# Packing the 64-row tails of a top-k attention and Fourier mixing kernel into shared 128-wide blocks, on one Trainium2 core

## The chip, the cores and the metric

The kernel runs on one core of one Trainium2 chip. The time is the device time of one execution in microseconds (us). Before the change the median of four runs is 2020.8 us (2019.78 to 2022.19). One execution was also taken with the hardware profiler; its rows carry the durations used below.

## The reference, cut to what matters

There are 8 batches of 8 heads, 576 positions and 64 features per head, all in float32. Each query keeps its 32 largest scores; then come a softmax, a product with `v`, a real Fourier mix over positions and channels, a layer norm and a two-layer MLP.

```python
scores = scale * np.matmul(q, k.transpose(0, 1, 3, 2))
kth = np.partition(scores, -top_k, axis=-1)[..., -top_k:-top_k + 1]
scores = np.where(scores >= kth, scores, -1000000000.0)
attn = np.exp(scores - np.max(scores, axis=-1, keepdims=True))
attn = attn / (np.sum(attn, axis=-1, keepdims=True) + 1e-09)
x = heads_side_by_side(np.matmul(attn, v))        # (8, 576, 512)
mixed = np.real(np.fft.fft(np.fft.fft(x, axis=1), axis=2))
u = x + mixed
ch = np.maximum(layer_norm(u) @ w_ch1, 0.0) @ w_ch2
return u + ch
```

## The kernel before

**Tiles.** 576 positions are four full blocks of 128 and a tail of 64 (32 rows from each half of the sequence). Two heads are handled together as a pair, one in partitions 0 to 63 and the other in 64 to 127 of the transposed `q` and `k`; there are 32 pairs, four per batch. A pair has nine *items* (`IN_PAIR`, L259): for each full query block one item for each head (`e` 0 and 1), and one item with the 64 tail queries of both heads stacked to 128 rows (`e` None). That makes 288 items.

**One item** passes these stations. TensorE (PE) makes its scores in PSUM (`scores`, L267: part 0 against the 512 full keys, one matmul per head, L296; part 1 against the 64 tail keys of both heads at once through the block-diagonal `kt_t`, L285), and ScalarE (ACT) copies them to an `S` tile (L299, L289). VectorE (DVE) finds the 32 largest with four MAX8 and three MATCH_REPLACE8 (L313, L315). GpSimd (POOL) makes the two bounds from them (`bounds`, L322). ACT makes a penalty with a Relu that reads the bound (L329), POOL subtracts it (L330); both are `mask`. ACT takes the exponential (L336). PE transposes the result in blocks of 128 columns (`transposes`, L355: four blocks and then one more for the tail, in a PSUM tile of its own), ACT copies the blocks to `PT` (L357), and for every 5 or 4 items PE multiplies with `v` (`attend`, L371).

**The loop.** `while` at L915 runs one step per item, and everything is issued in the order written there. In step i PE makes the scores of item i+3, spreads in *units* of the MLP of the previous batch (`hidden`, L659; `back`, L674 and L699), and transposes item i-2. DVE does the last rounds of item i and the first of item i+1. POOL gets `bounds(i)` (L1006), then what the plan put under "pool" (L1013), and in the next step the subtraction of item i. In the first 36 steps (the first batch) latencies are shorter by one step, no MLP is there yet, and DVE, ACT and POOL also convert the weights.

**Folds.** Before the Fourier matmuls of a batch (`dft_tokens`, L506) the rows of `x` are folded by four operations for each of two parities (`fold_ops`, L446, all through L462). For batches 1 to 6 they are on POOL, under "pool": one operation per step from step T0 and from T0+6 (L844), for batch 1 two per step from T0 and T0+3 (L837). The matmuls of parity 0 follow at T0+5 (T0+3 for batch 1).

**Preparation.** `prep` (L232) transposes `q` of the next pair at step 0 of a pair and `k` at step 5, each in five blocks, the last with 64 rows and zeros. Both come through the one `nat_t` buffer, loaded on SyncE's queue (SP) by L215 and L217. In the first batch `prep` uses the PSUM tiles "mm" (three banks, shared with the weight conversion); scores use "sp" (two banks).

**End of the MLP.** `back` leaves a block in PSUM; ACT scales it into `ct` (L680, a tile of the `W` ring that also holds the items' working rows), POOL adds it to `x` (L682; DVE in the last batch), SP stores it (L686). The 64-row tail block ends on DVE one step later (L713, L714).

`level` and `fixed_cost` (L873 to L891) share the MLP units out over the steps by an estimate of the PE time of each step.

Of the kernel before, what the change touches and what calls it, by code (L numbers as in the profile page):

```python
# [59 lines left out]
def kernel(  # L60
# [60 lines left out]
    kt_t = const.tile([P, P], F32, name="kt", tag="kt")  # L121
# [78 lines left out]
    nat, qT_of, kT_of, v_of, PT, Ssb, Wk, M8, Nt = ({} for _ in range(9))  # L200
# [5 lines left out]
    def load_heads(dst, src, pair, tail0=0, queues=None):  # L206
        b, hp = divmod(pair, NPB)
        for tails in range(2):
            queue = (queues or (nc.sync, nc.sync))[tails]
            for e in range(2):  # L210
                s2 = src[b, 2 * hp + e].rearrange("(h r) d -> h r d", h=2)
                for h in range(2):
                    r0 = tail0 + TH * h
                    if tails:
                        queue.dma_start(out=dst[r0:r0 + TH, NF, e, :], in_=s2[h, 2 * P:HS, :])  # L215
                    else:
                        queue.dma_start(  # L217
                            out=dst[:, 2 * h:2 * h + 2, e, :],
                            in_=s2[h, 0:2 * P, :].rearrange("(t p) d -> p t d", p=P),
                        )  # L220

    def load_nat(n, pair, dst=None, queues=None):
        if pair < NPAIR:
            nat[n, pair] = nat_t if dst is None else dst
            load_heads(nat[n, pair], q if n == "q" else k, pair, 0, queues)

    def load_v(pair):
        if pair < NPAIR:
            v_of[pair] = v_t[pair % 2]
            load_heads(v_of[pair], v, pair, TAIL)  # L230

    def prep(n, pair, pool=ps_t, tag="tp"):  # L232
# [5 lines left out]
        for c0, c1 in ((0, NF), (NF, NC)):  # L238
# [5 lines left out]
            if c0 == 0:  # L244
                dst, got = t_sb[:, 0:NF * P], tp.rearrange("p a c -> p (a c)")
            else:
                dst, got = t_sb[:, NF * P:], tp[:, 0, 0:TAIL]
            if n == "q":
                nc.scalar.mul(out=dst, in_=got, mul=scale)
            elif c0 == 0:  # L250
                nc.scalar.copy(out=dst, in_=got)
            else:
                for hd in (slice(0, D), slice(D, P)):
                    nc.scalar.copy(out=kt_t[hd, hd], in_=got[hd])
# [12 lines left out]
    def scores(i, part):  # L267
# [7 lines left out]
        rows, keys = ROWS[t], slice(0, NF * P)  # L275
        if part == 0:
            for n in range(1 if e is None else 2):
                Ssb[i + n] = attp.tile([P, S], F32, name=f"S_{i + n}", tag="S", bufs=6)

        to = [(Ssb[i], slice(TAIL * h, TAIL * (h + 1))) if e is None  # L280
              else (Ssb[i + h], slice(0, P)) for h in range(2)]
        q_cols = slice(P * t, P * t + rows)
        if part == 1:
            sp = ps_s.tile([P, NF * P], F32, name=f"sp_{i}_t", tag="sp")
            nc.tensor.matmul(  # L285
                sp[0:rows, 0:P], lhsT=qT[:, q_cols], rhs=kt_t, start=True, stop=True
            )
            for h, (s_t, r) in enumerate(to):
                nc.scalar.copy(  # L289
                    out=s_t[r, NF * P:S], in_=sp[0:rows, TAIL * h:TAIL * (h + 1)]  # L290
                )
            return 0.3
        for h, (s_t, r) in enumerate(to):
# [8 lines left out]
    def top_ops(i, rounds):  # L302
# [3 lines left out]
        if i not in Wk:  # L306
            Wk[i] = attp.tile([P, S], F32, name=f"wk_{i}", tag="W", bufs=5)
            M8[i] = small.tile([P, TOPK], F32, name=f"m8_{i}", tag="m8", bufs=5)
# [9 lines left out]
    def bounds(i):  # L318

        if i < N:  # L320
            Nt[i] = small.tile([P, 2], F32, name=f"nt_{i}", tag="nt", bufs=6)
# [19 lines left out]
    def transposes(i):  # L341
        pair, t, e = items[i]
        p_sb = Wk.pop(i)
        ch, col = CHUNK_OF[t]
        if (pair, ch) not in PT:
            PT[pair, ch] = attp.tile(
                [P, 2, NC, CW[ch]], F32, name=f"PT_{pair}_{ch}", tag=f"PT{ch}", bufs=1
            )
        pt = PT[pair, ch]
        dsts = [(e, 0, P)] if e is not None else [(0, 0, TAIL), (1, TAIL, TAIL)]  # L350
        for c0, c1 in ((0, NF), (NF, NC)):
            tp = ps_t.tile([P, 4, P], F32, name=f"tpP_{i}_{c0}", tag="tp")
            for c in range(c0, c1):
                k0 = min(P * c, S - P)
                nc.tensor.transpose(tp[:, c - c0, :], p_sb[:, k0:k0 + P], ident)  # L355
            for he, o, w in dsts:
                nc.scalar.copy(  # L357
                    out=pt[:, he, c0:c1, col:col + w], in_=tp[:, 0:c1 - c0, o:o + w]
                )
        return 0.6  # L360

    def attend(pair, ch, c0=0, c1=None):
# [6 lines left out]
        for c in range(NC):  # L369
            for e in range(2):  # L370
# [3 lines left out]
                    rhs=pt[:, e, c, c0:c1],  # L374
# [5 lines left out]
    def attended(pair, ch, late):  # L380
# [14 lines left out]
        rd = small.tile([P, 6], F32, name=f"rd_{pair}_{ch}", tag="rd", bufs=6)  # L395
# [205 lines left out]
    def stats(b, t):  # L601
        rows, mvb = ROWS[t], mv[b % 2]
        st6 = small.tile([P, 6], F32, name=f"st6_{b}_{t}", tag="st6")
# [44 lines left out]
    def mlp_units(b):  # L648
        x = x_of[b]
        last = b == B - 1  # L650
        hTs = {}

        def hidden(ch, it):
            w, unT = CW[ch], unT_of[b, ch]
            if ch not in hTs:
                hTs[ch] = batp.tile([P, NIT, CW[0]], F32, name=f"hT_{b}_{ch}", tag="hT")
            hp = ps_m.tile([P, CW[0]], F32, name=f"hp_{b}_{ch}_{it}", tag="mm")
# [5 lines left out]
            nc.scalar.activation(out=hTs[ch][:, it, 0:w], in_=hp[:, 0:w], func=AF.Relu)  # L663

        cps = {}

        def back(ch, t, part):
            n, hT, rs = CHUNKS[ch].index(t), hTs[ch], rs_of[b]
# [3 lines left out]
            if t != 4:  # L672
# [5 lines left out]
                if part == 7:  # L678
                    ct = attp.tile([P, DM], F32, name=f"ct_{b}_{t}", tag="W", bufs=5)
# [375 lines left out]
```

## Time and profile before

| what | value |
|---|---|
| median of four runs | 2020.8 us |
| the profiled execution | 2020.43 us |
| its span in the trace | 2018.7 us |
| PE busy | 1890.4 us (94%) |
| DVE busy | 1626.8 us (81%) |
| ACT busy | 1225.3 us (61%) |
| POOL busy | 852.2 us (42%) |
| L355 transposes of P on PE | 1440, mean 286 ns |
| L357 copies to PT on ACT, 128x128 form | 256, mean 278 ns |
| L296 scores of tail queries, 64x512 form | 128, mean 688 ns |

PEld is the loading of weights into TensorE, which overlaps PE. A row that begins with a line number is a group of equal instructions: line, engine, operation, output from input, count, then total busy time and the mean of one. In rows of the timeline the first two numbers are start and duration in us. "A <- B" in a list of waits means that A could go on when B had ended. A matmul in float32 shows as two records.

### The profile page before, as it was taken

To read this page: it belongs to the slowest core of one execution; us is meant where nothing else is said; L and a number is where in the kernel's file an instruction comes from. 1 tells how busy PE (TensorE), PEld (TensorE's weight loads), DVE (VectorE), ACT (ScalarE), POOL (GpSimd) and SP (SyncE) were. 2 spreads that over 40 slices of the span, in tenths; PEclk is the share of its full clock that TensorE was granted. 3 is DMA by queue.
4 is the path that set the end of the run, shared out by engine and by line. 5 is a ranking of instruction groups with operands and counts; after the bars stand their busy time and mean duration, and the time that the engine had idled before them with its cause. 6 is when DMAs were issued, how large, how long until landed. Compare 5 with 4: busy or idle time off the path is not lost.

```text
span 2018.7 us, 27736 instructions
## 1 busy us (share of the span) xinstructions
PE 1890.4 (94%) x8642; PEld 1142.9 (57%) x8642; DVE 1626.8 (81%) x3374; ACT 1225.3 (61%) x3059; POOL 852.2 (42%) x1143
## 2 busy tenths in 40 slices
PE   5667689999899999999999999999999999998999
PEld 3434356565565566647565656647565656556655
DVE  7998898999899999989889888888889888853100
ACT  6877737676676667657666666656666666651111
POOL 4869822334733265224632464225632454223100
PEclk8777679999899999999999999999999999999999
DMA  4323100010000100000000001000000001000000
GB/s 129 97 84 95 54 7 19 24 26 24 23 19 24 27 24 24 18 23 21 24 24 13 26 18 29 18 24 22 22 24 24 20 13 35 1 13 1 11 14 11
DMA packets 133587, 57.84 MB, mean 29 GB/s; under 512 B 124352, under 2 KB 124480, under 8 KB 133440
## 3 DMA queue, kind: packets, MB, share of 16 engines
q1 hardware_dynamic: 132208, 55.73, 10.2%
q8 instruction: 70, 1.15, 0.2%
q14 instruction: 77, 0.63, 0.1%
q10 hardware_dynamic: 1232, 0.33, 0.1%
HBM read 46.57 MB, written 9.44 MB: 28 GB/s over the span
## 4 chain that ended last, share of the span: by engine, by line
PE 78%; DVE 7%; ACT 5%; POOL 5%; issue 4%; DMA 0%; SPq 0%; POOLq 0%; DVEq 0%; ACTq 0%
PE hp L659 23%; PE cp L674 20%; PE o L371 7%; PE sp L296 7%; PE tpP L355 6%; PE mp L576 3%; PE yp L520 3%; PE cp L699 3%; DVE m L313 3%; DVE wk L315 2%; PE sp_t L285 2%; POOL wk L330 2%; POOL w L192 1%; PE cm L801 1%; ACT wk L336 1%
## 5 line engine op out<-in xcount | busy, mean ns | idle before, releaser
L330 POOL TENSOR_TENSOR wk<-S,wk 128x576 f32<-128x576 f32 x288 | 406.6, 1412 | 865.6 <-ACT wk L329 775.2
L313 DVE MAX8 m<-wk 128x8 f32<-128x576 f32 x864 | 623.1, 749 | 5.6
L659 PE MATMUL hp<-unT,w 128*128 128x256 f32 (+1 forms) x2048 | 538.6, 410 | 2.2 <-POOL t L625 2.2
L674 PE MATMUL cp<-w,hT 128*128 128x512 f32 x1024 | 479.2, 599 | 0.0
L659 PEld LDWEIGHTS hp<-unT,w 128*128 128x128 f32 x2048 | 374.5, 191 | 126.6 <-issue 31.8
L315 DVE MATCH_REPLACE8 wk<-m,wk 128x576 f32<-128x576 f32 x576 | 427.6, 742 | 0.0
L357 ACT COPY PT<-tpP 128x512 f32<-128x512 f32 (+3 forms) x640 | 221.4, 408 | 128.3 <-PE tpP L355 125.2
L674 PEld LDWEIGHTS cp<-w,hT 128*128 128x128 f32 x1024 | 179.4, 190 | 189.7 <-issue 188.9
L336 ACT ACTIVATE wk<-wk,nt 128x576 f32<-128x576 f32 x288 | 226.2, 785 | 78.3 <-POOL wk L330 77.1
L355 PE MATMUL tpP<-ident,wk 128*128 128x128 f32 x1440 | 219.7, 286 | 53.2 <-ACT wk L336 47.8
L355 PEld LDWEIGHTS tpP<-ident,wk 128*128 128x128 f32 x1440 | 173.7, 146 | 152.0 <-ACT wk L336 71.7
L313 DVE MAX8 m<-S 128x8 f32<-128x576 f32 x288 | 214.2, 744 | 36.9 <-ACT S L289 36.5
L329 ACT ACTIVATE wk<-S,nt 128x576 f32<-128x576 f32 x288 | 227.3, 789 | 10.5 <-POOL nt L322 8.7
L663 ACT ACTIVATE hT<-hp 128x320 f32<-128x320 f32 (+1 forms) x256 | 104.6, 409 | 194.3 <-PE hp L659 193.0
L299 ACT COPY S<-sp 128x512 f32<-128x512 f32 (+1 forms) x320 | 173.9, 586 | 74.2 <-PE sp L296 72.9
L315 DVE MATCH_REPLACE8 wk<-m,S 128x576 f32<-128x576 f32 x288 | 213.6, 742 | 0.0
L371 PE MATMUL o<-PT,v 128*64 128x256 f32 (+3 forms) x1440 | 196.9, 417 | 10.0 <-ACT PT L357 9.7
L296 PE MATMUL sp<-kT,qT 64*128 64x512 f32 (+1 forms) x640 | 198.4, 683 | 1.8 <-ACT means L811 1.7
L371 PEld LDWEIGHTS o<-PT,v 128*64 128x64 f32 x1440 | 111.7, 153 | 84.9 <-issue 15.0
L192 POOL TENSOR_TENSOR w<-w,space 128x512 f32<-128x512 f32 x96 | 123.5, 1286 | 5.9 <-ACT space L183 3.4
L682 DVE TENSOR_TENSOR x<-x,ct 128x512 f32<-128x512 f32 x4 | 2.8, 692 | 130.9 <-ACT ct L680 130.9
L420 DVE TENSOR_TENSOR x<-tpx,rd 128x256 f32<-128x256 f32 x64 | 27.2, 424 | 82.7 <-PE tpx L416 77.0
(111 smaller groups left out, 1737.3 us busy)
## 6 DMA issues: line engine op xcount, KB each, us to landing
space<-in_moe_w_ch_dram SPq DMA_DIRECT2D x32, 512.0 KB, 3.5
nat<-in_q_dram SPq DMA_DIRECT2D x128, 64.0 KB, 2.0
v<-in_v_dram SPq DMA_DIRECT2D x128, 64.0 KB, 2.1
out_dram<-x SPq DMA_DIRECT2D x32, 256.0 KB, 2.1
nat<-in_k_dram SPq DMA_DIRECT2D x124, 64.0 KB, 2.0
nat<-in_q_dram SPq DMA_DIRECT2D x128, 8.0 KB, 1.7
v<-in_v_dram SPq DMA_DIRECT2D x128, 8.0 KB, 1.7
nat<-in_k_dram SPq DMA_DIRECT2D x124, 8.0 KB, 1.6
```

What stands on the lines that cost most here:

```text
L296: nc.tensor.matmul(sp[r], lhsT=qT[hd, q_cols], rhs=kT[hd, :], start=True, stop=True)
L299: nc.scalar.copy(out=s_t[r, keys], in_=sp[r])
L313: ops.append(lambda src=src, m8=m8: nc.vector.max(out=m8, in_=src))
L315: ops.append(lambda src=src, m8=m8: nc.vector.match_replace(w, m8, src, NEG))
L329: nc.scalar.activation(out=w, in_=Ssb[i], func=AF.Relu, scale=-FAR, bias=Nt[i][:, 1:2])
L330: nc.gpsimd.tensor_tensor(out=w, in0=Ssb.pop(i), in1=w, op=ALU.subtract)
L336: nc.scalar.activation(out=w, in_=w, func=AF.Exp, bias=Nt.pop(i)[:, 0:1], accum_out=den_t[pair % 3][:, c:c + 1],)
L355: nc.tensor.transpose(tp[:, c - c0, :], p_sb[:, k0:k0 + P], ident)
L357: nc.scalar.copy(out=pt[:, he, c0:c1, col:col + w], in_=tp[:, 0:c1 - c0, o:o + w])
L371: nc.tensor.matmul(o[D * e:D * (e + 1), c0:c1], lhsT=vv[:, c, e, :], rhs=pt[:, e, c, c0:c1], start=(c == 0), stop=(c == NC - 1),)
L659: nc.tensor.matmul(hp[:, 0:w], lhsT=w1[:, dt, P * it:P * (it + 1)], rhs=unT[:, dt, 0:w], start=(dt == 0), stop=(dt == NDT - 1),)
L674: nc.tensor.matmul(cp, lhsT=hT[:, it, P * n:P * (n + 1)], rhs=w2[:, it, :], start=(it == 0), stop=(it == NIT - 1),)
```

## The change

The change has seven parts.

1. *P tails of two heads.* The working rows of the two items (t, 0) and (t, 1) lie side by side in one tile, `[P, 2, S]`, three buffers instead of five single ones. The second head's scores are stored with the 64 tail keys first. So the tails of both heads are 128 adjacent columns, transposed as one block when the second head's item is done. `PT` has 9 blocks instead of 10; the tail halves of `v` are placed to match, with zeros in the other half.
2. *Tails of q and k.* The 64 tail rows of `k` are loaded below those of `q`, by the loads for `q`; one transposed block gives both. `kt_t` has two copies. `k` is left with four blocks.
3. *Tail queries' scores.* Instead of two matmuls with 512 columns there are four with 256, on the four quarters of the PE array (64 rows by 64 columns); ACT copies four pieces instead of two.
4. *Folds.* Under a new name "pool0" they are issued ahead of `bounds(i)` instead of behind it. Those of parity 0 move one step later, for batch 1 those of both parities.
5. *End of the MLP.* `ct` leaves the `W` ring for the fold buffer "fold_s" and for free columns of `hT`, which is packed closely for the shorter chunk. The block t = 3 (and all of the last batch) is finished by one DVE instruction from PSUM, for batches 0 to 6 one step later.
6. *First batch.* `prep` takes its PSUM tiles from "sp" instead of "mm".
7. *Smaller rings* for `m8` (5 to 3), `nt` (6 to 4), `rd` (6 to 4) and `st6` (4 to 2), and changed costs in `fixed_cost`.

```diff
...
+            if n == "q":
+                load_tails(nat[n, pair], q, pair, (0, 0))
+                load_tails(nat[n, pair], k, pair, (TAIL, TAIL))
...
-            load_heads(v_of[pair], v, pair, TAIL)
+            load_full(v_of[pair], v, pair)
+            load_tails(v_of[pair], v, pair, (0, TAIL))
...
-        for c0, c1 in ((0, NF), (NF, NC)):
+        for c0, c1 in ((0, NF), (NF, NC)) if n == "q" else ((0, NF),):
...
+                nc.scalar.mul(out=t_sb[:, NF * P:], in_=got[:, 0:TAIL], mul=scale)
                 for hd in (slice(0, D), slice(D, P)):
-                    nc.scalar.copy(out=kt_t[hd, hd], in_=got[hd])
+                    nc.scalar.copy(out=kt_t[pair % 2][hd, hd], in_=got[hd, TAIL:P])
...
+        if e is None:
+            half = NF * P // 2
+            sps = [
+                ps_s.tile([P, NF * P], F32, name=f"sp_{i}_{h}", tag="sp") for h in range(2)
+            ]
+            for g in range(2):
+                for h in range(2):
+                    hd = slice(D * h, D * (h + 1))
+                    nc.tensor.matmul(
+                        sps[h][TAIL * g:TAIL * (g + 1), 0:half],
+                        lhsT=qT[hd, q_cols], rhs=kT[hd, half * g:half * (g + 1)],
+                        start=True, stop=True,
+                    )
+            for h, (s_t, r, _, _) in enumerate(to):
+                for g in range(2):
+                    nc.scalar.copy(
+                        out=s_t[r, half * g:half * (g + 1)],
+                        in_=sps[h][TAIL * g:TAIL * (g + 1), 0:half],
+                    )
+            return 0.6
...
-            Wk[i] = attp.tile([P, S], F32, name=f"wk_{i}", tag="W", bufs=5)
-            M8[i] = small.tile([P, TOPK], F32, name=f"m8_{i}", tag="m8", bufs=5)
+            e = items[i][2]
+            if e != 1:
+                Wp[i] = attp.tile([P, 2, S], F32, name=f"wk_{i}", tag="W", bufs=3)
+            Wk[i] = Wp[i - 1][:, 1, :] if e == 1 else Wp[i][:, 0, :]
+            M8[i] = small.tile([P, TOPK], F32, name=f"m8_{i}", tag="m8", bufs=3)
...
+        def full():
+            k0 = TAIL if e == 1 else 0
+            tp = ps_t.tile([P, 4, P], F32, name=f"tpP_{i}", tag="tp")
+            for c in range(NF):
+                nc.tensor.transpose(tp[:, c, :], p_sb[:, k0 + P * c:k0 + P * (c + 1)], ident)
...
+        def tails():
+            tp = ps_t.tile([P, 4, P], F32, name=f"tpP_{i}_t", tag="tp")
+            if e == 1:
+                both = Wp.pop(i - 1).rearrange("p e s -> p (e s)")[:, NF * P:S + TAIL]
+                nc.tensor.transpose(tp[:, 0, :], both, ident)
+                nc.scalar.copy(out=pt[:, 2 * NF, col:col + P], in_=tp[:, 0, :])
+                return
...
+        full()
+        if e != 0:
+            tails()
+        return 0.48 if e == 0 else 0.6
...
-                    rhs=pt[:, e, c, c0:c1],
+                    rhs=pt[:, 2 * NF if c == NF else NF * e + c, c0:c1],
...
+                    def finish():
+                        nc.vector.scalar_tensor_tensor(
+                            out=xt, in0=cp, scalar=rs[:, t:t + 1], in1=xt, op0=ALU.mult, op1=ALU.add
+                        )
+
+                    if last:
+                        finish()
+                    elif t == 3:
+                        late_next.append(finish)
+                    else:
+                        ct = ct_of(t)
+                        nc.scalar.mul(out=ct, in_=cp, mul=rs[:, t:t + 1])
+                        nc.gpsimd.tensor_tensor(out=xt, in0=xt, in1=ct, op=ALU.add)
...
-                        at(T0 + 3 * par + n // 2, "pool", op)
+                        at(T0 + 3 * par + n // 2 + 1, "pool0", op)
...
-                        at(T0 + 6 * par + n, "pool", op)
+                        at(T0 + (6 if par else 1) + n, "pool0", op)
...
-        preps, bank = [], (ps_m, "mm") if short else (ps_t, "tp")
+        preps, bank = [], (ps_s, "sp") if short else (ps_t, "tp")
...
+        run(i, "pool0")
         bounds(i)
```

## The prediction, made before the changed kernel was run

> **What bounds the kernel now.** I read four views in this order: busy time by stage, the waits of the engine that looks full, the chain that ended last (for the price of one operation), and POOL's timeline (for what is moved). By stage, the columns are start:end and length, then busy us (and instructions) of PE, PEld, DVE, ACT and POOL, then the granted TensorE clock:
>
> ```profile
> 0.00:280.00 280.00, 182.07 (x784) 106.64 (x785) 252.12 (x524) 205.18 (x471) 201.49 (x197) 0.74 0.28 84
> 280.00:500.00 220.00, 215.41 (x1020) 131.58 (x1019) 208.47 (x436) 142.65 (x366) 66.09 (x95) 0.99 0.09 21
> 500.00:545.00 45.00, 37.97 (x175) 22.63 (x174) 39.50 (x79) 26.31 (x71) 35.30 (x54) 0.89 0.11 26
> 545.00:1800.00 1255.00, 1246.94 (x5900) 749.36 (x5898) 1098.26 (x2286) 813.45 (x2061) 525.17 (x758) 1.00 0.09 21
> 1800.00:2019.00 219.00, 208.00 (x770) 132.67 (x768) 28.41 (x53) 37.73 (x91) 24.15 (x41) 0.98 0.03 10
> ```
>
> The reader sees five stages. Up to 280 us (first batch) DVE is full and PE is not. From 545 to 1800 us PE is full and DVE has 12% to spare. 500 to 545 holds the folds of batch 1: nobody is full, and the clock falls to 0.89. After 1800 only the last MLP is left. That PE really works from 545 to 1800 is said by its waits there (total us, times, longest):
>
> ```profile
> PE tpq L241 <- ACT PT L357: 2.0, 5, 0.4
> PE tpP L355 <- ACT wk L336: 1.9, 3, 0.8
> PE tpk L241 <- ACT PT L357: 1.9, 1, 1.9
> ```
>
> These are the longest three of five, which sum to 8 us in 1255. So what PE saves there comes off the end, nearly one for one. POOL's subtraction L330 counts 205 in this stage, so it holds 205 items or 22.8 pairs, at 6.12 us per item.
>
> **Part by part.** *Price of a transpose.* On the chain of waits of 1040 to 1056 us:
>
> ```profile
> 1040.35 1.06 PE sp L296 x4
> ...
> 1043.76 0.33 PE tpx L416 x3
> 1044.08 0.55 PE tpP L355 x5
> ...
> 1047.01 0.55 PE tpk L241 x5
> ...
> 1049.71 0.22 PE tpx L416 x2
> ```
>
> Two, three and five transposes hold PE for 0.22, 0.33 and 0.55 us: 0.11 us each, with no fixed part. The group's mean of 286 ns is the life of one in a pipeline, not what one costs. (The Trainium skill says the same in "Trainium Kernel Development and Optimization", section Performance Expectations: matmul busy time is a bad metric because matmuls are pipelined. With 286 ns the transposes below would be priced 2.6 times as high.)
>
> *P tails and k tail (parts 1 and 2).* Per pair four items of the first head lose one transpose each, and `prep` of `k` loses one: 5 x 0.11 = 0.55 us of PE per pair. ACT loses four 128x128 copies (278 ns) per pair and pays three small ones instead of two for the stacked item, about +0.1 us; ACT is at 65% in the PE stage, so I count this as nothing. If ACT were full it would be 1.0 us per pair more gain.
>
> *Tail queries' scores (part 3).* Today two matmuls of 64x64 against 512 columns, four records, hold PE from 909.62 to 910.63:
>
> ```profile
> 907.20 0.77 PE L355 MATMUL tpP<-ident,wk 128*128 128x128 f32 x5
> 907.80 1.89 PE L659 MATMUL hp<-unT,w 128*128 128x256 f32 x8
> 909.62 1.07 PE L296 MATMUL sp<-kT,qT 64*64 64x512 f32 x4
> 910.63 1.35 PE L659 MATMUL hp<-unT,w 128*128 128x256 f32 x5
> ```
>
> That is 1.0 us. `hp` shows 8 records of 256 columns in 1.82 us, 0.23 each; so one of 512 alone would be 0.46 and four 1.8 us: the two heads already run beside each other. No row has four quarters at work. If all four run together, 8 records x 0.23 / 4 = 0.46 us plus some 0.1 us to fill: 0.4 to 0.55 saved. If only two do, as in `attend` (20 records of 256 in 2.31 us), it is 0.92: 0.1 saved. If the eight weight loads (142 ns for the 64x64 form) came one after the other it is 1.1: 0.1 lost. I take 0.45 saved, since both pairings, two row halves here and two column halves in `attend`, are seen to run together; ends -0.1 and 0.6. ACT pays four copies of 64x256 (370 ns by the 128x256 xT row) for two of 576: +0.3 us per pair, under the same cover.
>
> (The Trainium skill, "TensorEngine Tiling (Array Packing)", section Instruction Overhead, speaks against it: about 60 cycles for each matmul, so shorter ones waste more. No row here isolates that. With its 2.4 GHz, four more records would be an estimated 0.1 us per pair, 2.3 us in the sum.)
>
> So 0.55 + 0.45 = 1.0 us of PE per pair. From 545 to 1800: 22.8 x 1.0 = **22.8 us** (ends 0.45 and 1.15: 10 to 26). From 280 to 545 there are 44 items, 4.9 pairs, but DVE is at 95% and 88%: half, **2.4 us** (0 to 4.9). Up to 280 us PE's saving is worth nothing.
>
> *First batch (part 6).* DVE's weight split L165 waits 7.2 us in all for the copies of `qT` and `kT`, with which it shares the banks "mm". That goes; the same copies can now hold up the scores in "sp", where DVE's MAX8 waits only 1.8 us for S after the start. I take **3 us** gain (7 gained to 6 lost: eight copies of 0.6 and some small ones).
>
> *Last block (part 5).* At the very end ACT's 0.69 and DVE's 0.69 us become one DVE instruction (0.86 by L714): **0.6 us**. In batches 0 to 6 ACT loses 0.69 and POOL 1.27 us, DVE gains 0.86 seven times, covered by its 12%; the PSUM bank is held until DVE gets there, and of three "mm" banks two stay.
>
> *Folds (part 4).* Here POOL in batch 2:
>
> ```profile
> 714.95 1.42 POOL L330 TENSOR_TENSOR wk<-S,wk 128x576 f32<-128x576 f32 x1 [0.71 <-ACT wk L329]
> 716.32 0.20 POOL L322 TENSOR_TENSOR nt<-m,cc 128x2 f32<-128x2 f32 x1
> 716.47 3.87 POOL L462 TENSOR_TENSOR zw<-sd 128x512 f32<-128x512 f32 x4
> 720.30 1.41 POOL L330 TENSOR_TENSOR wk<-S,wk 128x576 f32<-128x576 f32 x1
> ```
>
> The bound (L322) starts as soon as the subtraction before it ends: DVE had it ready. POOL's idle time lies behind the bound, before the next subtraction, where it waits for ACT's Relu (598 us of waits from 545 to 1800). The folds now fill just that gap. Ahead of the bound they hold up the bound, so the Relu of that item, and behind it in ACT's order the evictions of `hp`, the copies to PT and the exponential. A loop of one step becomes Relu 0.79 + subtraction 1.41 + fold 3.87 + bound 0.19 + some 0.2 of handing over = 6.5 us against a step of 6.12; for the first operation, with its wait for ACT's copy (18.6 us over 13 folds, 1.4 each), 2.36 + 1.4 + 1.26 = 5.0 and so 7.6; the last two (2.7 each) give it back. So a Relu is late by at most 1.9 us per run of folds. From the end of an exponential to its transposes the timeline of 900 to 925 us shows 2.9 us or more (909.98 to 912.91), so most is absorbed. But parity 0 is a step later with its matmuls left in place: they now need the fold in the step after it, where there was one to spare. I take 0.4 us for five batches. Batch 1, two operations per step (loops of 10.1 and 7.6 us), stands still already (PE idle 7 us, clock loss 5 us) and I add 2. **4 us lost**; ends: 12 gained (that stall goes) and 33 lost (all of 10 x 1.9, 5 x 2 and 4 reach PE).
>
> *At nothing.* SP: four `k` tail loads move to `q`'s turn, 12 issues of about 0.5 us instead of 8, with `v`'s eight and stores behind them; `q` is needed four steps (24 us) later, so 2 us of delay are hidden. The rings: MAX8 into `m8` now waits for the bound three items back, some 5 us earlier in the trace. The `W` pairs: DVE can run one step ahead of PE, not more; a wait like today's L315 <- L355 (24.1 us in 23 waits) would come twice in nine items, and DVE has 0.7 us per item to cover it.
>
> **Sum.** 22.8 + 2.4 + 3 + 0.6 - 4 = 24.8 us off the profiled execution's 2020.4 (span 2018.7 and 1.7 around it) gives 1995.6. The median of the runs is 0.4 higher: **1996 us**.
>
> **Rivals.** (1) *DVE becomes the bound*, 2008 us: 9 x 5.36 us of DVE work (1098 / 205), two new W waits of 2.2 and 2 us of waits for tpx are 54.6 us per pair, against PE's 55.1 - 1.0 = 54.1; some of the rest is lost in the handovers and half the gain stays. For: 208 of 220 us busy in the second stage. Against: DVE runs ahead. (2) *Folds reach PE*, 2025 us, the slower side: 33 lost instead of 4, against 28.8 gained. It decides where more than 28.8 / 12 = 2.4 us per run of folds reach PE. For: the timelines show ACT and POOL doing their work in the order of the code, so what is behind a late bound waits too. Against: 2.9 us of slack and three "mm" banks. (3) *The stall of batch 1 goes*, 1980 us: 12 gained instead of 4 lost; against it, POOL has the same work in the same steps. (4) That the quarters don't run together is inside the forecast's own range: 0.35 x 27.7 pairs, 10 us, 2006.
>
> **How the numbers follow.** Forecast 0.60 (1986 to 2006), rival 1 0.16, rival 2 0.16, rival 3 0.08. The range from 1980 to 2014 leaves out rival 2 and a little more. A measurement of this kernel tells some 0.2%, 4 us, from no change. Of rival 2's 0.16 I give 0.03 to within that bound and 0.13 to slower; the rest, 0.84, is faster.
>
> **What would show it.** Right: 1312 transposes at L355's successor instead of 1440 (128 fewer), 128 instead of 160 for `k`, still 0.11 us apart; the tail scores in about 0.55 us; the stage of 22.8 pairs shorter by some 23 us with PE still without waits. Wrong: DVE waiting on PE's transposes in every pair and PE on exponentials (rival 1); ACT's Relu waiting for the bound by tens of us and PE's waits growing in the fold steps (rival 2); PE at full clock through batch 1's folds (rival 3).

## The result, and the profile after

The changed kernel takes **2024.5 us** (median of 38 runs, 2021.4 to 2030.9) against 2021.2 for the kernel before beside it (56 runs, 2019.3 to 2022.9). The ratio is 1.0019, with a 95% interval of 1.0014 to 1.0024: **slower by 0.2%**, where 1.2% faster was forecast. The profiled execution took 2023.2 us, with a span of 2021.3.

The same five stages as before, with the same columns:

```profile
0.00:280.00 280.00, 174.57 (x759) 102.04 (x760) 245.46 (x507) 204.70 (x465) 201.00 (x198) 0.71 0.28 84
280.00:500.00 220.00, 212.82 (x1025) 131.12 (x1025) 210.06 (x442) 142.24 (x361) 64.70 (x94) 0.98 0.09 21
500.00:545.00 45.00, 33.74 (x132) 18.35 (x130) 33.64 (x70) 20.87 (x54) 29.32 (x41) 0.81 0.07 15
545.00:1800.00 1255.00, 1244.32 (x5946) 749.46 (x5947) 1108.76 (x2316) 819.70 (x2058) 526.89 (x768) 1.00 0.09 22
1800.00:2019.00 219.00, 206.94 (x753) 131.10 (x751) 30.53 (x49) 32.35 (x80) 22.63 (x40) 0.96 0.02 7
```

What is to be seen is where less gets done. In the first 280 us DVE is busy for 245 us instead of 252, and DVE is what bounds that stage. From 500 to 545 us PE is busy for 33.7 instead of 38.0 us, at a clock of 0.81 instead of 0.89. From 545 to 1800 PE is as full as before and issues more instructions (5946 against 5900): there the change works. At the end PE idles more.

The prices of single operations came out as forecast. This is PE's timeline:

```profile
918.72 0.60 PE L392 MATMUL tpP<-ident,wk 128*128 128x128 f32 x4
919.25 0.66 PE L312 MATMUL sp<-kT,qT 64*64 64x256 f32 x8
919.85 1.99 PE L720 MATMUL hp<-unT,w 128*128 128x256 f32 x8
...
923.96 0.60 PE L392 MATMUL tpP<-ident,wk 128*128 128x128 f32 x4
924.40 0.27 PE L403 MATMUL tpP_t<-ident,wk 128*128 128x128 f32 x1
924.51 1.68 PE L720 MATMUL hp<-unT,w 128*128 128x256 f32 x7
```

From start to next start, four transposes hold PE for 0.44 us (923.96 to 924.40), the pair's tail block for 0.11, and the eight records on the four quarters for 0.60 us (919.25 to 919.85) where four records took 1.01 before. So the quarters do run together. Per pair PE is spared 5 x 0.109 + 0.413 = 0.96 us; 1.0 was forecast.

I follow the loss item by item: the start of POOL's subtraction (L365) of each of the 288 items, less its start in the kernel before (L330). The change is behind by 6.2 us at item 27, by 12.5 at item 82 (just after batch 1's folds), ahead by 1.6 at item 287 and behind by 2.6 at the end. So it loses in two places in the first 550 us, wins 14 us in the stage where PE is full, and loses 4 us in the tail.

### The profile page after: what moved, and what is told of

Read it like the earlier page. It is cut to its first block, busy times and chain, and to the rows that moved or that the text cites. A ratio compares the mean times of both kernels' runs of the same rounds, so it can differ in the third digit from the quotient of the medians.

```text
span 2021.3 us, 27569 instructions
## 1 busy us (share of the span) xinstructions
PE 1872.4 (93%) x8610; PEld 1132.1 (56%) x8610; DVE 1628.4 (81%) x3381; ACT 1219.9 (60%) x3016; POOL 844.5 (42%) x1137
## 4 chain that ended last, share of the span: by engine, by line
PE 74%; DVE 13%; ACT 5%; POOL 5%; issue 2%; DMA 0%; SPq 0%; DVEq 0%; POOLq 0%; ACTq 0%
PE hp L720 23%; PE cp L744 20%; PE o L429 7%; DVE m L348 5%; PE tpP L392 5%; PE sp L327 5%; DVE wk L350 4%; PE yp L578 4%; PE cp L780 3%; PE mp L634 2%; PE sp_t L297 2%; POOL wk L365 2%; POOL w L192 1%; PE cm L884 1%; ACT wk L371 1%
## 5 line engine op out<-in xcount | busy, mean ns | idle before, releaser
L365 POOL TENSOR_TENSOR wk<-S,wk 128x576 f32<-128x576 f32 x288 | 406.7, 1412 | 883.4 <-ACT wk L364 833.7
L395 ACT COPY PT<-tpP 128x512 f32<-128x512 f32 (+1 forms) x320 | 170.8, 545 | 123.7 <-PE tpP L392 121.5
L392 PE MATMUL tpP<-ident,wk 128*128 128x128 f32 x1152 | 187.9, 288 | 44.8 <-ACT wk L371 44.4
L392 PEld LDWEIGHTS tpP<-ident,wk 128*128 128x128 f32 x1152 | 142.3, 147 | 145.6 <-ACT wk L371 67.2
L330 ACT COPY S<-sp 128x512 f32<-128x512 f32 x256 | 137.1, 588 | 67.9 <-PE sp L327 67.5
L327 PE MATMUL sp<-kT,qT 64*128 64x512 f32 x512 | 161.7, 687 | 3.0 <-ACT means L894 1.9
L758 DVE SCALAR_TENSOR_TENSOR x<-cp,gi,x 128x512 f32<-128x512 f32 x11 | 8.2, 746 | 128.3 <-PE cp L744 128.3
L297 PEld LDWEIGHTS sp_t<-kt,qT 128*128 128x128 f32 (+1 forms) x322 | 52.1, 189 | 63.3 <-ACT S L319 23.6
```

What stands on the lines that cost most here:

```text
L327: nc.tensor.matmul(sp[r], lhsT=qT[hd, q_cols], rhs=kT[hd, :], start=True, stop=True)
L365: nc.gpsimd.tensor_tensor(out=w, in0=Ssb.pop(i), in1=w, op=ALU.subtract)
L392: nc.tensor.transpose(tp[:, c, :], p_sb[:, k0 + P * c:k0 + P * (c + 1)], ident)
L395: nc.scalar.copy(out=pt[:, NF * he:NF * (he + 1), col:col + w], in_=tp[:, :, o:o + w])
```

## The experiments

Eighteen kernels, each timed beside the kernel before on the same chip (2020.4 to 2021.4 us there). The figure in the last column is the difference of the medians from that.

| run | kernel | median us | less before |
|---|---|---|---|
| e1 | after, part 4 undone | 2014.0 | -7.1 |
| e2 | after, part 6 undone | 2011.5 | -9.6 |
| e3 | after, parts 4 and 6 undone | 2006.0 | -15.1 |
| e4 | after, folds behind the bound, steps as in after | 2023.9 | +2.7 |
| e5 | before + part 6 | 2032.8 | +11.6 |
| e6 | before + part 4 | 2028.3 | +7.2 |
| e7 | before + part 3, without its costs | 2014.3 | -6.8 |
| e8 | e3 with before's costs | 1999.6 | -21.5 |
| e9 | before, folds behind the bound, a step later | 2028.9 | +8.5 |
| e10 | e8, block t = 3 not on DVE | 2001.4 | -19.0 |
| e11 | e8, first batch's blocks in "tp" | 2002.0 | -18.4 |
| e12 | e8 with both of these | 2001.5 | -18.9 |
| e13 | e9 and Fourier matmuls a step later | 2029.3 | +7.9 |
| e14 | e8, batch 1 laid out like batches 2 to 6 | 2010.7 | -10.7 |
| e15 | after, Fourier matmuls a step later, "mm", old costs | 2008.5 | -13.0 |
| e16 | e8 with only the scores' new cost | 1999.0 | -22.5 |
| e17 | before, second half of batch 1's mixing a step later | 2024.3 | +3.1 |
| e18 | e8, that half a step earlier | 1995.5 | -25.7 |

### Which part costs: e1, e2, e3, e4

```diff
# e1: part 4 undone
-                        at(T0 + 3 * par + n // 2 + 1, "pool0", op)
+                        at(T0 + 3 * par + n // 2, "pool", op)
...
-                        at(T0 + (6 if par else 1) + n, "pool0", op)
+                        at(T0 + 6 * par + n, "pool", op)
# e2: part 6 undone
-        preps, bank = [], (ps_s, "sp") if short else (ps_t, "tp")
+        preps, bank = [], (ps_m, "mm") if short else (ps_t, "tp")
```

e3 has both edits. e4 only renames "pool0" to "pool", so that the folds stand behind the bound in the later steps.

e1: 

> The changed kernel with part 4 alone undone: the folds again behind the bound, in the steps of before. Theory A (the folds ahead of the bound hold up the bound, so ACT's Relu and with it PE; the trace of the changed kernel shows 9 us more PE standstill from 500 to 600 us and about 7 us more from 600 to 1800): 2024.5 - 12 to 16 = 2009 to 2013 us, ACT's waits for the bound fall from 50 us to under 12. Rival B (the loss comes from the shorter rings and the W pairs, which make DVE wait): 2022 to 2025 us, DVE's waits for the bound and for PE's transposes stay near 35 and 45 us.

e2: 

> The changed kernel with part 6 alone undone: in the first batch the transposes of q and k use the PSUM tiles mm again. Theory A (in the tiles of the scores they hold up the scores: items 23 and 27 each come 3.7 us later than before): the first 280 us get back 4 to 6 us, 2019 to 2021 us. Rival B (the loss of the first batch lies in the start, where tails of q and k are loaded first, 1.7 us, and in ACT): at most 2 us, 2022.5 to 2024.5 us.

e3: 

> The changed kernel with parts 4 and 6 undone. If both theories A hold and the losses add: 2004 to 2009 us, so faster than before by 0.6 to 0.85%. If rival B holds for both: 2020 to 2024 us. If only one part costs: 2009 to 2021 us.

e4: 

> The changed kernel with the folds behind the bound but in the later steps of the changed kernel (parity 0 one step later, for batch 1 both parities): tells the place from the delay. If the place ahead of the bound is what costs (theory A1): as with the folds fully back, 2009 to 2013 us. If the Fourier matmuls now wait for folds that are a step late (theory A2): 2018 to 2025 us, with PE waiting for fg on POOL before the Fourier matmuls.

Part 4 costs 10.5 us (e1 against after) or 5.5 (e2 against e3), part 6 costs 13.0 or 8.0, together 18.5. After and e1 scatter more than the kernel before (after from 2021.4 to 2030.9, the five runs of e1 from 2011.7 to 2018.5), so each of these prices is known to some 3 us, and the 5 us between the two orders are hardly more than that. In after's own trace the folds look like the second rival of the prediction:

```profile
510.84 3.85 POOL L520 TENSOR_TENSOR zw<-sd 128x512 f32<-128x512 f32 x4
514.66 0.18 POOL L357 TENSOR_TENSOR nt<-m,cc 128x2 f32<-128x2 f32 x1
514.87 0.78 ACT L364 ACTIVATE wk<-S,nt 128x576 f32<-128x576 f32 x1 [5.80 <-POOL nt L357]
515.55 0.56 ACT L253 COPY kT<-tpk 128x512 f32<-128x512 f32 x1
516.17 0.33 PE L403 MATMUL tpP_t<-ident,wk 128*128 128x128 f32 x1 [3.56 <-ACT kT L253]
```

The fold ends, the bound follows, the Relu has waited 5.8 us for it, the copy of kT stands behind the Relu, and PE has waited 3.6 us for that copy. But this is not what most of the loss comes from. In e4 the bound is ahead of the folds again, the Relu's waits for it (43.8 us from 300 to 1800 in after) are no longer among the nine longest of ACT, the last of which is 7.8, and 9.9 of 10.5 us stay lost (to some 3 us: e4's twelve runs lie between 2019.4 and 2027.4). So with the later steps the place adds little, and theory A1 fell. No run has the folds ahead of the bound in their old steps.

### The terms alone, on the kernel before: e5, e6, e7

e5 and e6 are the same edits as in part 6 and part 4, made in the kernel before. e7 takes over part 3, with the planner's costs left alone:

```diff
+        if e is None:
+            half = NF * P // 2
...
+            for g in range(2):
+                for h in range(2):
...
+                    nc.tensor.matmul(
+                        sps[h][TAIL * g:TAIL * (g + 1), 0:half],
+                        lhsT=qT[hd, q_cols], rhs=kT[hd, half * g:half * (g + 1)],
...
+            return 1.04
```

e5: 

> The kernel before with part 6 alone: the blocks of q and k of the first batch go through the banks of the scores (sp) instead of mm. Theory A (the move costs by itself: taking it back was worth 13.0 us in after and 8.0 us with the folds back): 2029 to 2034 us, and the loss is all there by item 40. Rival B (it costs only beside the rest of the change, the later tail loads and the shorter PE order): within 4 us of 2021. My prediction's own term said a gain of 3: 2018.

e6: 

> The kernel before with part 4 alone: folds ahead of the bound and in the later steps, rings of five and six buffers as before. Theory A (the lateness and the place cost by themselves; taking them back was worth 10.5 us in after and 5.5 us with the bank back): 2026 to 2032 us, with the Fourier matmuls or the Relu waiting for POOL in batch 1. Rival B (only the ring of three m8 buffers turns a late bound into a wait of DVE; it was 35 us of waits in after and none before): 2020 to 2024 us, DVE without waits for the bound.

e7: 

> The kernel before with part 3 alone: the tail queries' scores on four quarters, the unit costs of the planner left as they were, so no unit moves. Theory A (PE time saved in the stage where PE is full comes off the end one for one: 0.41 us in each of 22.8 pairs there and half of it in 4.9 pairs before): 2010 to 2013 us. Rival B (a part is handed back in new waits of PE, as in the kernel with folds and bank back, where 14.3 of 21.9 us came off): 2014 to 2017 us.

**The bank (e5)** costs 11.6 us by itself. All of it is there by item 40 (+11.3) and nothing is added afterwards. First the kernel before, then e5, the same blocks of `k` in both timelines:

```profile
165.71 0.48 PE L241 MATMUL tpk<-ident,nat 128*128 128x128 f32 x1 [1.77 <-ACT w L177]
165.98 5.55 PE L801 MATMUL cm<-w,ones 128*128 128x512 f32 x8
172.01 0.88 ACT L357 COPY PT<-tpP 128x256 f32<-128x256 f32 x4 [2.02 <-PE tpP L355]
```

```profile
169.03 0.48 PE L241 MATMUL tpk<-ident,nat 128*128 128x128 f32 x1 [4.20 <-ACT S L289]
170.63 5.47 PE L801 MATMUL cm<-w,ones 128*128 128x512 f32 x8 [1.11 <-ACT kT L251]
176.57 0.88 ACT L357 COPY PT<-tpP 128x256 f32<-128x256 f32 x4 [5.67 <-PE tpP L355]
178.64 0.70 DVE L162 TENSOR_SCALAR wm<-space 128x512 int32<-128x512 int32 x1 [5.28 <-ACT w L177]
```

"sp" has two banks, and three users now take them in turn: the scores, `prep`, and `cm`, the centring of the weights. `tpk` waits 4.2 us until ACT has copied the last scores (L289), which in ACT's order stands behind the weight work and the exponential. From 20 to 330 us `tpq` and `tpk` wait 28.2 us in e5 for such copies. `cm` then waits for the copy of kT. `cm` holds PE for 5.5 us whatever comes, so ACT waits 5.7 us for P behind it, and the bounding engine DVE waits 5.3 us for ACT's weight step. In the kernel before this step of DVE (at 175.26 us) did not wait. From 20 to 330 us DVE's waits sum to 28.7 us in e5 and to 17.1 before: 11.6 more, which is the whole loss. No run moves `cm` or the scores alone, so their shares are not told apart. The prediction asked only how long the scores would be held up (MAX8 waits) and never listed who else lives in those banks.

**The folds (e6)** cost 7.2 us by themselves. The loss is 6.6 us at item 82, 8.3 at 120 and 8.7 at 287: nearly all comes in batch 1, and five batches add 2 us. It comes although the rings still have five and six buffers, so rival B fell.

**The quarters (e7)** win 6.8 us: 2014.3 is past theory A's range and at the near edge of rival B's. To see why I summed, for items 90 to 279, the time from each group's first start on PE to the next group's. The `sp` groups shrink by 7.7 us in 21 pairs, 0.37 each. But in 7 of the 21 pairs the group that follows the quarters lasts 0.35 us longer (2.25 instead of 1.91 us for `cp`), 2.4 us in all or 0.11 per pair. These groups now end in a wait of `sp_t` for its bank, which the waits of PE from 600 to 1790 us list and those of the kernel before did not:

```profile
PE sp_t L285 <- ACT S L308: 1.9, 7, 0.3
```

`sp_t` takes the bank of the first head, which is free when ACT has copied that head's two pieces of 365 ns, 0.73 us in all, instead of one of 576 ns. PE also comes to it 0.41 us earlier, and in five of the seven cases ACT has a copy for a fold (`sd`, 0.62 us) just ahead. The copy that I had put "under the same cover" stands on PE's way through a ring of two banks. The rows show 1.9 of those 2.4 us; that the rest is the same wait is argued.

### The planner's costs: e8 and e16

```diff
-        t = 0.55 if 0 <= i - 2 < N else 0.0
+        t = 0.6 if 0 <= i - 2 < N else 0.0
...
-            t += {0: 1.04, 1: 0.3, None: 0.9}[items[i + 3][2]]
+            t += {0: 1.04, 1: 0.3, None: 1.34}[items[i + 3][2]]
...
-        return 0.48 if e == 0 else 0.6
+        return 0.6
```

The value returned by `scores` for the tail item goes back from 0.6 to 1.04 as well. e16 puts back only the two lines on transposes (the first and the last).

e8: 

> After with parts 4 and 6 undone, and the planner's costs put back to those of before (0.6, 1.34, 1.04), so that the MLP units stand in the same steps as before. Theory A (the new costs move the units: one hp unit less is left to cover the last normalise, which costs 4 us at the end, and some of the 7 us that items 82 to 287 fall short): 1998 to 2003 us. Rival B (the shortfall comes of the W pairs and the part 5 and the tail of chance in the order): 2004 to 2008 us, like its parent at 2006.0.

e16: 

> After with parts 4 and 6 undone and the planner's cost of the transposes put back, that of the tail queries' scores left at its new value. Theory A (0.4 us less in one step of nine lets the planner place more units there, as the main part of the new costs): 2004 to 2007 us. Rival B (0.05 to 0.12 us less in every step is more in sum, 0.6 us per pair, and moves more): 1998 to 2002 us.

The changed estimates cost **6.4 us** (2006.0 in e3, 1999.6 in e8), although no instruction is different and at item 276 the two stand within 1 us (17.9 and 17.0 ahead of before). It all comes after that. These are the last normalise, the fold and the first Fourier matmul of the last batch, in e3 and then in e8:

```profile
1813.01 0.42 DVE L478 TENSOR_TENSOR x<-tpx,rd 128x256 f32<-128x256 f32 x1 [18.78 <-PE tpx L474]
1818.76 5.12 DVE L520 TENSOR_TENSOR zw<-sd 128x512 f32<-128x512 f32 x4
1825.12 1.30 PE L578 MATMUL yp<-fs,fg 128*128 128x145 f32 x4 [8.71 <-DVE fg L520]
```

```profile
1811.30 0.42 DVE L478 TENSOR_TENSOR x<-tpx,rd 128x256 f32<-128x256 f32 x1 [17.05 <-PE tpx L474]
1816.00 4.08 DVE L520 TENSOR_TENSOR zw<-sd 128x512 f32<-128x512 f32 x4
1821.69 4.05 PE L578 MATMUL yp<-fs,fg 128*128 128x145 f32 x16 [5.26 <-DVE fg L520]
```

With the smaller costs the planner puts one more `hp` unit (1.7 us) ahead of the last transposes. The last normalise is 1.7 us later, and there is one unit less to do while DVE folds: PE idles for 8.7 us instead of 5.3. Nor does the folding take the same time. In e8 POOL's second fold step waits 1.5 us for an ACT copy, in e3 it does not, and there DVE's sums take 5.12 instead of 4.08 us. Theory A of e16 fell: the scores' cost does nothing (1999.0), and the 0.05 to 0.12 us off the transposes, in every step, is what moves that unit.

### Place, lateness or arrival: e9, e13, e15, e17

```diff
# e9, in before: later steps, still behind the bound
-                        at(T0 + 3 * par + n // 2, "pool", op)
+                        at(T0 + 3 * par + n // 2 + 1, "pool", op)
...
-                        at(T0 + 6 * par + n, "pool", op)
+                        at(T0 + (6 if par else 1) + n, "pool", op)
# e13: e9 and
-            ft, fc = (T0 + 3, T0 + 6), T0 + 7
+            ft, fc = (T0 + 4, T0 + 7), T0 + 8
# e17, in before
-            ft, fc = (T0 + 3, T0 + 6), T0 + 7
+            ft, fc = (T0 + 3, T0 + 6), T0 + 8
```

e15 is after with the edit of e13 in `ft, fc`, with part 6 undone (e2) and the old costs (e8).

e9: 

> The kernel before with the folds left behind the bound, but in the later steps of part 4. Part 4 alone cost 7.2 us in before. Theory A1 (the place ahead of the bound costs: the Relu waits for a bound that stands behind the folds): 2020 to 2023 us here. Theory A2 (the lateness costs: the Fourier matmuls stay in their step and now wait for the last fold): 2026 to 2030 us, with yp waiting for POOL's fold and no new waits of the Relu.

e13: 

> The kernel before with the folds behind the bound in the later steps (2028.9 us), and batch 1's Fourier matmuls and what follows them one step later too. Theory A (the wait of yp for the last fold is what costs): 2019 to 2023 us, yp without waits. Rival B (the later arrival and the other order of batch 1 cost): 2026 to 2030 us.

e15: 

> After with its folds ahead of the bound as they are, but batch 1's Fourier matmuls one step later, the first batch's blocks in mm again and the planner's old costs. Theory A (the place ahead of the bound costs next to nothing, the lateness did): 1998 to 2002 us, like the kernel with folds as before at 1999.6. Rival B (with m8 rings of three the bound behind the folds makes DVE wait in batch 1): 2003 to 2008 us, and DVE MAX8 waits for the bound by tens of us.

e17: 

> The kernel before with its folds and batch 1's first Fourier matmuls where they are; only the second half of the mixing (mp and what follows, so the arrival of batch 1's MLP units too) is one step later. Theory A (PE runs short of units before they arrive, and each step of delay costs): 2025 to 2030 us. Rival B (the steps in which the folds themselves stand are what costs): 2019 to 2023 us.

e9 settles the place for batch 1: without it the whole loss is 8.5 us, no less than the 7.2 of e6, and from item 72 to item 82 e9 loses 7.5 us and e6 6.9. In the five later batches it is otherwise: there the trace of e9 loses nothing more and that of e6 2.1 us, so the place has a small price there. In the waits of PE from 500 to 565 us the Fourier matmuls of e9 wait for the last fold:

```profile
PE yp L520 <- POOL fg L462: 9.6, 2, 5.9
```

I took that wait for the cause. e13 gives the matmuls their step back, and the wait goes, but the time does not come back. The same window of e13:

```profile
PE tpP L355 <- ACT wk L336: 4.6, 1, 4.6
PE tpP L355 <- ACT qT L249: 3.9, 1, 3.9
```

So PE stands still in the fold steps all the same, now at the transposes of P. That is a part of the loss; the rest shows in a wider window, with the granted clock beside it. These are 440 to 610 us of before, e9, e13 and e17, in the columns of the five stages:

```profile
440.00:610.00 170.00, 160.53 (x788) 99.91 (x788) 160.01 (x334) 114.60 (x296) 82.37 (x123) 0.97 0.08 20
440.00:610.00 170.00, 156.03 (x748) 98.45 (x748) 151.43 (x319) 111.31 (x287) 80.88 (x120) 0.94 0.08 20
440.00:610.00 170.00, 154.71 (x737) 94.96 (x734) 156.89 (x327) 108.28 (x282) 80.60 (x119) 0.95 0.08 20
440.00:610.00 170.00, 159.86 (x780) 99.82 (x780) 159.60 (x334) 113.57 (x293) 82.04 (x121) 0.96 0.08 20
```

PE is busy for 4.5 us less in e9, 5.8 in e13 and 0.7 in e17, and its clock is 0.03, 0.02 and 0.01 lower, which over 170 us is an estimated 5.1, 3.4 and 1.7 us more. The sums, 9.6, 9.2 and 2.4, come near the losses of 8.5, 7.9 and 3.1, to the 2 us that a clock of two places allows. So what is lost shows as idle PE and as a lower clock, in roughly like parts.

e15 shows the same on the changed kernel: 8.9 us over e8. Theory A of e15 falls. Rival B's sign is there, MAX8 waits 36.8 us for the bound from 300 to 1800 us, but e13 loses 7.9 us with the bound ahead of the folds and rings of five, so these waits are left with some 1 us, the two differences being known to about 2. e17 moves only what comes after the folds, and with it the arrival of batch 1's MLP units, by one step: 3.1 us. So a step of delay in batch 1 costs 3 us by the arrival, and 8 when the folds move too. **What stays open** is how the other 5 us come about: PE has little to fill its time with between the fold steps and the arrival, but I have no run that takes the fill alone, and none that tells whether the standstill brings the lower clock.

### What else was tried on e8: e10, e11, e12, e14, e18

```diff
# e10: t = 3 like the blocks 0 to 2
-            if t == 2:
-                return hTs[1].rearrange("p i c -> p (i c)")[:, NIT * CW[1]:NIT * CW[1] + DM]
+            if t in (2, 3):
+                c0 = NIT * CW[1] + DM * (t - 2)
+                return hTs[1].rearrange("p i c -> p (i c)")[:, c0:c0 + DM]
...
-                    elif t == 3:
-                        late_next.append(finish)
# e11
-        preps, bank = [], (ps_m, "mm") if short else (ps_t, "tp")
+        preps, bank = [], (ps_t, "tp")
# e14
-        elif soon:
+        elif False:
# e18
-            ft, fc = (T0 + 3, T0 + 6), T0 + 7
+            ft, fc = (T0 + 3, T0 + 6), T0 + 6
```

e10: 

> The kernel with parts 4 and 6 and the planner's costs undone (1999.6 us), and block t = 3 finished like the blocks 0 to 2 (ACT's product into free columns of hT, POOL's sum) instead of one DVE instruction a step later. Theory A (the PSUM bank that is held until DVE gets there delays PE by 0.3 us a time at most, seen in two waits of hp for the DVE line): 1998 to 2001 us, no difference. Rival B (it is behind the small stalls of 700 to 815 us and the 4 us that the stage of items 82 to 287 still lacks): 1994 to 1997 us.

e11: 

> The kernel at 1999.6 us, with the blocks of q and k of the first batch in the third kind of bank, tp, that the later batches use for them. Theory A (what makes the scores' banks dear is that cm and the scores share two of them with the transposes, in ACT's order; in tp the transposes wait only for copies of P): within 3 of 1999.6, since mm is not what bounds the first batch either. Rival B (any bank but mm makes PE wait for ACT in the first batch): 2004 to 2012 us. Rival C (mm costs the weight split its 7 us of waits, and they go): 1992 to 1996 us.

e12: 

> Both of the two edits before on the kernel at 1999.6 us. If they do not touch each other, the sum of their two differences; 1992 to 2001 us.

e14: 

> The kernel at 1999.6 us with batch 1's folds, one operation in a step, and its Fourier matmuls placed as in batches 2 to 6. Theory A (two fold operations in a step are what makes the standstill of 500 to 545 us; it goes, and some 7 to 10 us with it): 1989 to 1994 us. Rival B (its MLP units arrive 5 steps later and PE has too few units in the meantime, so a standstill comes of that): 2000 to 2012 us.

e18: 

> The kernel at 1999.6 us, with the second half of batch 1's mixing one step earlier, in the step of the second Fourier matmuls. Theory A (earlier arrival wins what later arrival costs): 1992 to 1997 us. Rival B (mp then waits for ACT's copies of y, as it has no step between): 1999 to 2004 us.

e10, e11 and e12 have ratios to before of 0.9906 to 0.9909 with intervals of 0.9893 to 0.9922; that of e8 is 0.9892 (0.9878 to 0.9905). The intervals overlap, so neither edit is told from nothing. Part 5's late DVE instruction costs nothing that can be seen. In the first batch "tp" does as well as "mm", so it is "sp" that is bad and not every bank but "mm"; with "tp" the wait of the weight split L165 for the copy of qT (2.8 us in e8) goes and nothing is won, so rival C fell too.

e14 costs 11.1 us. From 440 to 600 us PE is busy for 142.2 us there and 149.0 in e8, and DVE for 154.2 of the 160: with the arrival five steps later the same units are stretched over more steps, and PE has gaps in all of them. That DVE's pace is what is left there is my reading; in e8 DVE is busy for 151.8. e18 goes the other way and wins 4.1 us more, with **1995.5 us** the best kernel here: 0.9875 of before, 0.9859 to 0.9890. Its interval overlaps that of e8 too, but all its four runs (1993.7 to 1997.1) lie below all four of e8 (1997.3 to 2000.9).

## Why the prediction was wrong

The runs make a chain from before to after, one part at a time. Each number is the difference of two medians above.

| term | forecast us | measured us | from |
|---|---|---|---|
| part 3, quarters | -11.4 (0.45 x 25.3) | -6.8 | before to e7 |
| parts 1, 2, 5 and the rings | -14.5 (0.55 x 25.3, 0.6) | -14.7 | e7 to e8 |
| new costs in `fixed_cost` | no term | +6.4 | e8 to e3 |
| part 6, bank | -3 | +8.0 | e3 to e1 |
| part 4, folds | +4 | +10.5 | e1 to after |
| sum | -24.9 | +3.4 | |

(25.3 pairs are the prediction's 22.8 and half of 4.9. The last two terms are not additive: in the other order they are 13.0 and 5.5 us, and why there are 5 us between them, if it is more than scatter, is open. That -14.7 meets -14.5 is partly luck: in the traces e8 gains 10.3 us on e7 in items 82 to 287, where 12.5 was forecast, and the rest before and after.)

*What bounds the kernel: right.* What PE saves comes off the end, except where ACT's copies stand in between. e8 takes 21.5 of the 25.9 us that the PE terms and the end promised.

*Price of a transpose, P tails, k tail: right in mechanism and size.* The count is 1152 + 160 = 1312 as forecast, still 0.11 us apart.

*Tail queries' scores: right on PE, wrong on its cover.* 0.41 us saved, 0.45 forecast. The step that failed is "ACT pays four copies ... under the same cover": ACT as a whole has room, but its copies free a ring of two banks that PE needs next. Of the 4.6 us short, some 2.4 are these waits, 1.0 the size (0.04 x 25.3), and 1.1 was laid on the stage from 280 to 545 us, where e7 has gained nothing at item 82.

*First batch: wrong sign.* The step that failed is "I take 3 us gain". Its far end, 6 lost, was too near as well. The waits of L165 for the copies do go in e5, as said. What came instead are waits of PE, and then of DVE's weight steps, through banks shared with `cm`.

*Folds: right about the five later batches (2 us forecast, 2.1 in e6), wrong about batch 1 (2 forecast, 6.6 measured).* The step that failed is "I add 2", which goes by the loops of the bound's place: in batch 1 the later steps alone lose as much (e9: 7.5 us), with the bound ahead of the folds as before. The sentence that touched this, matmuls left in place with no step to spare, was priced at next to nothing. The wait that it speaks of is there, 9.6 us in e9, but it is not shown to be the cause, since e13 takes it away and wins back only 0.6 us. What the runs show in its place is PE idle for longer and at a lower clock in batch 1, in roughly like parts; what brings them about is open. The prediction's slower case, 2025 us, has the right time by luck: it lays 29 us more on the folds, and 6.5 of them are there (10.5 instead of 4). The rest came from the bank (11.0), the costs (6.4) and the quarters (4.6). The Relu does wait for the bound, 43.8 us from 300 to 1800, and little of this wait is paid.

*At nothing.* The `W` pairs: DVE waits for the tail transposes 54.0 us in e8 instead of 24.1 for the transposes of P before, and e8 has in sum the gain that parts 1, 2 and 5 were to bring, so this was right to about 2 us. The `m8` ring shows 35 us of waits in after, but e15 against e8 loses no more than e13 against before (8.9 and 7.9), so some 1 us is left for it, known to about 2. But the changed costs of part 7 were in the list of parts and in no step: that is 6.4 us that was never priced.

*The end:* 0.6 us forecast; e8 gains 1.9 us after item 287 on the kernel before, after loses 4.2 there, by the planner's `hp` unit.

*Rival 1* (DVE as the bound) did not come: in after DVE is busy 1108.8 of 1255 us in the PE stage, and PE 1244.3. *Rival 3* (the stall of batch 1 goes) did not either, and e14 shows that a slower order of the folds does not remove it.

## What to carry to other kernels

Before moving a tile to another ring of banks, list everyone who takes that ring in turn, the one-off users too, and whose engine order frees each bank: here `cm` and ACT's score copies together made 11.6 us out of a move meant for nothing but room. A planner's cost constant is part of a change like any instruction: look at what it places last, since after the last item a unit ahead of the final chain delays it, and a unit kept back covers it. A long row of waits is no price until a run without it is faster: the Relu's 43.8 us and the W ring's 54 cost some 2 us each at most as far as these runs tell, and taking away yp's 9.6 us only moved the standstill.

## What the runs showed of the hardware

- Four matmuls of 64x64 on the four quarters, eight records of 256 columns, held PE for 0.60 us. A single record of 256 columns holds it for 0.23 (`hp`), and 8 x 0.23 / 4 is 0.46, so the quarters run together, and 0.14 us on top holds whatever having more instructions costs.
- DVE's two-input sums slow down while POOL does such sums beside it. Four sums of 128x512 on DVE took 1.94 us in the kernel before at 276.80 us, when POOL was idle. Four of the same size (`zw`) took 4.08 us in e8, beside POOL's second fold step and then its own `zw`, and 5.12 in e3, beside POOL's `zw` nearly throughout:

```profile
276.80 1.94 DVE L462 TENSOR_TENSOR fsp<-fsp 128x512 f32<-128x512 f32 x4
```
